# Attention with a gated ReGLU branch on one core: query products of two nested Strassen levels, cut into wider units

## The chip, the core and the metric

The kernel runs on one core of a Trainium2 chip, as one program. Time is the device time of one execution in microseconds (us); a lower one is better. The engines of the core run side by side, each through its own queue in order, and wait for each other by semaphores: TensorE (PE, with its weight loads PEld), VectorE (DVE), ScalarE (ACT), GpSimd (POOL), and SyncE (SP), which only issues transfers.

## What is computed

```python
x = A_x                                        # 1 x 2048 x 512, bfloat16
xn = layernorm(x)
q = (xn @ wq).reshape(1, 2048, 32, 128)        # 32 heads of 128
p = softmax(q k_cache^T * 128 ** -0.5)         # per head, 2048 cached keys
s = concat_heads(p v_cache) @ wo               # 2048 x 512
gate = xn @ W_gate; up = xn @ W_up             # 512 x 1792
g = silu((gate * (gate > 0) * up) @ W_down)    # 2048 x 512
out = x + s * g
```

## The kernel before

**Attention loop.** Work is ordered by pairs. A *pair* is two tiles of 128 keys against 512 queries of one head: two score matmuls (L1455, 512 columns each) into a two-bank PSUM slot, one exponential on ScalarE over both (L1467), and eight value matmuls (L1564, 129 columns) that accumulate into `ps_acc`. Eight pairs make a *block* (one head, one quarter Q of the queries), four blocks a head, and four heads a *group*: 16 blocks, 8 groups, 128 blocks in all. In the text r is a block's place in its group of 16, 0 to 15, and p0 to p7 are the pairs of a block. TensorE issues the scores of a pair three pairs ahead of its value matmuls (`LAG`). Value matmuls wait for the exponential of their pair. At the end of a block VectorE normalises (L1484, L1487), and SP issues the transpose of the result into `OT_store` (L1492); the first value matmul of the next block waits for the normalisation.

**Ring.** PSUM has three slots of two banks (`ps_r`, `NSLOT`). `ring_acquire` takes them in turn for score pairs and for all other products, and TensorE waits until the last reader of a slot is done: the exponential, or VectorE. A slot can be held (`hold=True`): it then leaves the turn until `ring_release` puts it back as second next, with the tokens that its next user waits for.

**Side work.** What else has to be done is hung on pairs by tables at the end of the program: `plan` (TensorE work of a pair, put between its score matmuls and its value matmuls) and `side` (work of other engines, emitted after it). In a pair without `plan` work the order is one score matmul, four value matmuls, the other score matmul, four value matmuls. The side work of the steady groups is:
- Output projection of the group before (`emit_os`, products on L1336, additions into `s_acc` on L1354): one step in p0 of each block; steps of two products in three blocks of four, and in r = 3, 7, 11, 15 a step of one product, where the scores of the next pair are pulled ahead of it (`early`). Before it, VectorE forms four sums of `OT_store` into `OX` twice a group: in r=0, p2 to p5, and in r=7, p1 to p4 (`emit_ox`, L1305 to L1313). GpSimd prepares `Wo` (`emit_wx`, L1278 and L1289 to L1294) in r=6, p0.
- Query projection of the next group. Heads are projected four at a time by Strassen's scheme applied twice: seven outer products (j = 1 to 7), each again by seven inner ones. The outer order is 1, 2, 6, 5, 3, 7, 4. A *unit* is one outer product for half of the columns (c = 0 or 1): seven matmuls of 256 columns (L1030). There are 14 units a group, for groups 2 to 7; groups 0 and 1 are projected by the one-level scheme (`emit_st`).

**A unit.** GpSimd forms the inner sums ahead (`prep_unit`, L1005): four tiles T of the activations, of the tile set TI, and four tiles X of the weights, of SI; it waits until the unit two before is done, whose tiles these are. Then five steps in consecutive pairs p3 to p7 of one block, on one held slot with banks A and B (`emit_unit`): TensorE writes a product into A or B, mostly accumulating onto what stands there, and VectorE reads the bank in between and adds it to the running sums UU, VV, RR (L1035, or a copy on L1034) or writes finished query tiles to `QT_sb`. The next product into a bank waits for that reading. At step 1 one read of A goes into two quarters at once (`to_broadcast`), except in units 1 and 5, which start new sums. The units j=5 and j=7 are followed by sums on GpSimd (`add_unit`, L1098 and L1104), which the next unit's first addition waits for.

**Weights.** `load_unit_w`, `scale_unit_w` and `sum_unit_w` bring and prepare the weights of a group in r = 2 and 4 (L979 to L991).

**Gate.** The gated branch is computed at the start, beside the first 16 blocks; its result g stands in `g_sb` (16 KB a partition) until the last group, where `emit_base` (from block 117 on, L1432 and L1437) multiplies and adds the input tiles that `issue_xr` has loaded from block 116 on.

**Start.** The first products of the one-level scheme (`emit_st`, pr=0, c=1, step 0) are read out by a copy on ScalarE (L908), since ScalarE is used there and VectorE elsewhere (L911); the result goes on to L898.

Of the kernel before, what the change touches and what calls it, by code (L numbers as in the profile page):

```python
# [52 lines left out]
def bass_recurrent_scan__mha_block_cached__glu_gated_reglu__prompt_kernel(  # L53
# [63 lines left out]
    with ExitStack() as es:  # L117
# [18 lines left out]
        xnT = S_([128, DC, S], BF16, "xnT")  # L136
        g_sb = S_([128, NT, D], BF16, "g_sb")
# [112 lines left out]
        sem_ui = newsem()  # L250
        sem_up = newsem()
# [15 lines left out]
        sem_qpa = newsem()  # L267
# [605 lines left out]
        def emit_st(pr, c, step, *banks):  # L873
# [26 lines left out]
            if step == 0:  # L900
                _wait(pe, sw_tok[(pr, 0)])
                if pr == 0 and c == 0:
                    _wait_all(pe, xt_ready[0])
                p1 = prod(1, banks[0])
                p2 = prod(2, banks[1])
                if pr == 0 and c == 1:
                    _wait_all(act, [p1, st_tok["r"]])
                    st_tok["u"] = sem_qpa.sig(act.copy(cu[:], ps_r[:, banks[0], :]))  # L908
# [29 lines left out]
        unit_order = (1, 2, 6, 5, 3, 7, 4)  # L938
        unit_at = []
# [17 lines left out]
        def outer_x(j, i, c, r):  # L957
            a = c * NQ + r * HQ
            if j == 1:
                return xnT[:, i, a:a + HQ]  # L960
            if j == 2:
                return xnT[:, HC + i, a:a + HQ]
            if j == 3:
                return xnT[:, HC + i, HS + a:HS + a + HQ]
            return TX[:, {5: 0, 6: 1, 7: 2, 4: 3}[j], i, a:a + HQ]

        def load_unit_w(g, i):
# [3 lines left out]
            else:  # L971
                _wait(sp, u_done[(g - 1, 1, 4 if i else 2)])
# [8 lines left out]
        def sum_unit_w(g):  # L981
            _wait(pool, wu_tok[(g, 1)])
            _wait(pool, u_done[(g - 1, 1, 7)] if g > 2 else qp_done_tok[3])
# [9 lines left out]
        def prep_unit(n):  # L993
            g, c, j, _ = unit_at[n]
            T, X = TI[n % 2], SI[n % 2]
            if n >= 2:
                _wait(pool, u_done[unit_at[n - 2][:3]])
# [3 lines left out]
            b11, b12 = outer_x(j, 0, c, 0), outer_x(j, 0, c, 1)  # L1001
            b21, b22 = outer_x(j, 1, c, 0), outer_x(j, 1, c, 1)
# [4 lines left out]
            k1 = op(T[:, 0], b12, b11)  # L1007
            k2 = op(X[:, 0], a21, a22, ALU.add)
            op(T[:, 2], b22, b12)
            op(X[:, 2], a11, a21)  # L1010
            _wait(pool, k1)
            k3 = op(T[:, 1], b22, T[:, 0])
# [3 lines left out]
            op(T[:, 3], b21, T[:, 1])  # L1016
# [3 lines left out]
        def emit_unit(n, step):  # L1020
            g, c, j, _ = unit_at[n]
# [18 lines left out]
            outs = {2: (0, c), 3: (0, c + QB // 2), 4: (2, c)}.get(j)  # L1040
            k = u_tok

            def out(i):
# [3 lines left out]
                hq = (G * g + outs[0] + e, outs[1])  # L1047
                if hq not in qt_slot:
                    qt_take(*hq)
                return QT_sb[qt_slot[hq]][:, r * HQ:(r + 1) * HQ]  # L1050

            def outdone(tok):
                if outs is not None:
                    for e in range(2):
                        qt_ready[(G * g + outs[0] + e, outs[1])] = tok

            if step == 0:
                p1 = mm(A, outer_w(j, 0, 0), outer_x(j, 0, c, 0), True, False)
                p6 = mm(B, X[:, 1, :], T[:, 1, :], True, False)
# [6 lines left out]
            elif step == 1:  # L1066
                _wait(pe, k["b"])
                p5 = mm(B, X[:, 0, :], T[:, 0, :], False, False)
# [3 lines left out]
                else:  # L1072
                    k["b"] = dv(D[3], base[:, 3, :], B, p5)
                    k["a"] = dv(dest[:, 2:4, :], dest[:, 2:4, :],
                                ps_r[:, 2 * s:2 * s + 1, 0:HQ].to_broadcast([128, 2, HQ]), k["b"])
            elif step == 2:
                _wait(pe, k["b"])
                p3 = mm(B, X[:, 3, :], outer_x(j, 1, c, 1), False, True)
                k["b"] = dv(out(1), D[1], B, p3, k["a"])
            elif step == 3:  # L1080
                _wait(pe, k["a"])
                p2 = mm(A, outer_w(j, 1, 0), outer_x(j, 1, c, 0), False, True)
                _wait(pe, k["b"])
                p7 = mm(B, X[:, 2, :], T[:, 2, :], True, False)
                k["b"] = dv(out(3), D[3], B, p7, k["a"])
                k["a"] = dv(out(0), None if base is None else base[:, 0, :], A, p2)
            else:
                _wait(pe, k["b"])
                p4 = mm(B, outer_w(j, 1, 1), T[:, 3, :], False, True)
                u_done[(g, c, j)] = p4  # L1090
                k["last"] = dv(out(2), D[2], B, p4, k["a"])
# [3 lines left out]
        def add_unit(g, c, j):  # L1095
            _wait(pool, u_tok["last"])
            if j == 5:
                u_tok["add"] = sem_uv.sig(pool.tensor_tensor(VV[:], UU[:], RR[:], ALU.add))  # L1098
                return
            for e in range(2):  # L1100
# [738 lines left out]
```

## Time and profile before

| | us |
|---|---|
| median of three runs | 1244.05 |
| their range | 1243.62 to 1244.43 |
| the profiled execution, its time | 1243.37 |
| the profiled execution, its span | 1242.0 |
| TensorE busy | 1224.3 |
| ScalarE busy | 1032.0 |
| VectorE busy | 858.9 |
| GpSimd busy | 694.4 |
| granted TensorE clock, mean | 1.0 |

The span is the time from the first to the last instruction. In the views below a row is a group of like instructions or, in the timeline, a run of them on one engine: start, time from its first start to its last end, engine, line, operation, tiles written and read, shapes and count; brackets give the idle time of the engine before it and what ended that. Matmuls are pipelined: the time from one start to the next is what one costs, and their own durations overlap. A busy time of TensorE therefore doesn't say how much it could still take.

### The profile page before, as it was taken

What the parts mean: (1) busy time and instruction counts of PE and PEld (TensorE: products, weight loads), DVE (VectorE), ACT (ScalarE), POOL (GpSimd) and SP (SyncE); (2) the same over time, 40 slices, a digit from 0 to 9 for tenths busy, and PEclk for the clock granted to TensorE, in tenths of its full rate; (3) what the DMA queues carried; (4) which work ended last, traced back from release to release, by engine and by line L of the source; (5) the groups of instructions that cost most, each with busy time, mean ns of one, the idle gap of its engine ahead of it and who ended that gap; (6) DMA issues with size and microseconds to landing.
All of it is one profiled execution on the core that took longest, in us unless ns stands there. A gap on an engine that the chain in (4) does not pass through costs nothing.

```text
span 1242.0 us, 30671 instructions
## 1 busy us (share of the span) xinstructions
PE 1224.3 (99%) x12413; PEld 890.9 (72%) x12647; DVE 858.9 (69%) x1664; ACT 1032.0 (83%) x1109; POOL 694.4 (56%) x930
## 2 busy tenths in 40 slices
PE   9999999999999999999999999999999999999998
PEld 5466666777777777777777777777777777777775
DVE  7677778666666766776766667667666676666667
ACT  4457877667898898988988988998989989889994
POOL 3383876414645578547864687457863796550002
PEclk9999999999999999999999999999999999999999
DMA  9712331221222232233122332242222223434312
GB/s 275 157 31 36 77 81 23 52 48 35 49 48 52 65 70 53 48 69 61 43 37 48 73 61 53 48 69 66 51 52 52 53 48 48 53 69 74 77 36 77
DMA packets 250699, 78.14 MB, mean 63 GB/s; under 512 B 226240, under 2 KB 250560, under 8 KB 250560
## 3 DMA queue, kind: packets, MB, share of 16 engines
q1 hardware_dynamic: 249888, 75.79, 31.2%
q8 instruction: 100, 1.64, 0.6%
q10 hardware_dynamic: 672, 0.39, 0.1%
q14 instruction: 39, 0.32, 0.1%
HBM read 38.54 MB, written 2.10 MB: 33 GB/s over the span
## 4 chain that ended last, share of the span: by engine, by line
PE 87%; issue 8%; ACT 3%; DVE 1%; POOL 1%; POOLq 0%; DVEq 0%
PE ps_acc L1564 33%; PE ps_r L1455 29%; PE ps_r L1336 6%; PE ps_r L1030 6%; PE ps_r L1133 3%; ACT PT L1467 3%; PE ps_r L1194 3%; PE ps_r L708 2%; PE ps_r L712 2%; PE ps_r L893 2%; PE ps_acc L811 1%; DVE UVR L1035 1%; POOL g_sb L1619 1%; PE ps_r L459 0%; PE ps_r L525 0%
## 5 line engine op out<-in xcount | busy, mean ns | idle before, releaser
L1467 ACT ACTIVATE PT<-ps_r 128x1024 bf16<-128x1024 f32 x1024 | 980.6, 1030 | 141.2 <-PE ps_r L1455 129.8
L1564 PE MATMUL ps_acc<-V_sb,PT 128*128 128x129 bf16 x8192 | 688.3, 220 | 5.4
L1564 PEld LDWEIGHTS ps_acc<-V_sb,PT 128*128 128x128 bf16 x8192 | 574.9, 98 | 145.2 <-ACT PT L1467 2.9
L1455 PE MATMUL ps_r<-QT_sb,KT_sb 128*128 128x512 bf16 x1823 | 600.8, 379 | 5.3 <-DVE QT_sb L898 0.3
L1035 DVE TENSOR_TENSOR UVR<-UVR,ps_r 128x256 f32<-128x256 f32 (+1 forms) x456 | 198.3, 455 | 160.8 <-PE ps_r L1030 156.1
L1354 DVE TENSOR_TENSOR s_acc<-s_acc,ps_r 128x512 f32<-128x512 f32 x264 | 167.8, 683 | 15.2 <-PE ps_r L1336 15.2
L1455 PEld LDWEIGHTS ps_r<-QT_sb,KT_sb 128*128 128x128 bf16 x2048 | 171.7, 98 | 7.6 <-ACT PT L1467 0.5
L1005 POOL TENSOR_TENSOR TI<-xn_sb 128x256 f16<-128x256 f16 x96 | 66.2, 689 | 89.0 <-PE ps_r L1030 88.1
L1487 DVE TENSOR_TENSOR Onorm<-ps_acc,rz_sb 128x512 bf16<-128x512 f32 x127 | 87.8, 692 | 4.4
L1098 POOL TENSOR_TENSOR UVR<-UVR,UVR 128x1024 f32<-128x1024 f32 x12 | 28.3, 2361 | 99.2 <-DVE UVR L1035 99.2
L1035 DVE TENSOR_TENSOR QT_sb<-UVR,ps_r 128x256 bf16<-128x256 f32 x144 | 57.4, 419 | 28.2 <-PE ps_r L1030 23.4
L1030 PE MATMUL ps_r<-TI,SI 128*128 128x256 f16 x252 | 68.7, 273 | 0.0
L1005 POOL TENSOR_TENSOR TI<-xn_sb,TI 128x256 f16<-128x256 f16 x96 | 67.6, 704 | 0.0
L1619 POOL TENSOR_TENSOR g_sb<-s_acc,WX 128x512 bf16<-128x512 f32 x6 | 6.8, 1155 | 108.0 <-DVE WX L1612 108.0
L1005 POOL TENSOR_TENSOR TI<-xnT 128x256 f16<-128x256 bf16 x72 | 50.7, 704 | 28.0 <-PE ps_r L1030 28.0
L1484 DVE RECIPROCAL rz_sb<-ps_acc 128x4 f32<-128x4 f32 x127 | 23.2, 183 | 61.7 <-PE ps_acc L1564 59.0
L979 POOL TENSOR_SCALAR Wq_sb<-Wq_sb 128x1024 bf16<-128x1024 bf16 x12 | 33.2, 2770 | 48.2 <-DMA Wq_sb<-in_A_wq_dram 46.9
L1104 POOL TENSOR_TENSOR QT_sb<-UVR,UVR 128x512 bf16<-128x512 f32 x24 | 30.1, 1276 | 38.7 <-DVE UVR L1035 38.7
L1034 DVE COPY UVR<-ps_r 128x256 f32<-128x256 f32 x72 | 28.2, 419 | 33.6 <-PE ps_r L1030 33.6
L1005 POOL TENSOR_TENSOR TI<-xnT,TI 128x256 f16<-128x256 bf16 x72 | 50.7, 704 | 0.0
L1030 PEld LDWEIGHTS ps_r<-TI,SI 128*128 128x128 f16 x252 | 24.3, 97 | 34.1 <-DVE QT_sb L1035 6.8
L1005 POOL TENSOR_TENSOR SI<-SO 128x128 f16<-128x128 f16 x96 | 48.6, 506 | 0.0
(186 smaller groups left out, 1342.7 us busy)
## 6 DMA issues: line engine op xcount, KB each, us to landing
V_sb<-in_A_v_cache_dram SPq DMA_DIRECT2D x32, 512.0 KB, 4.5
Wq_sb<-in_A_wq_dram SPq DMA_DIRECT2D x16, 256.0 KB, 3.2
Wo_sb<-in_A_wo_dram SPq DMA_DIRECT2D x8, 512.0 KB, 4.8
xr_sb<-in_A_x_dram SPq DMA_DIRECT2D x16, 128.0 KB, 2.0
OT_store<-Onorm SPq DMA_TRANSPOSE x127, 2.5
Wd_sb<-in_B_W_down_dram SPq DMA_DIRECT2D x1, 1792.0 KB, 14.1
W<-in_B_W_gate_dram SPq DMA_DIRECT2D x14, 128.0 KB, 2.4
W<-in_B_W_up_dram SPq DMA_DIRECT2D x14, 128.0 KB, 2.8
```

Of the source, the lines that this page charges most:

```text
L979: wu_tok[(g, i)] = sem_uo.sig(pool.tensor_scalar(w, w, WSC, None, op0=ALU.mult))
L1005: return sem_ui.sig(pool.tensor_tensor(dst, x, y, o))
L1030: return sem_up.sig(pe.matmul(dst, lhs, rhs, start=start, stop=stop, skip_group_check=True))
L1035: dve.tensor_tensor(dst, x, ps, ALU.add))
L1133: ins = pe.matmul(ps_r[:, bank, :], L(i), R(i), start=(i == 0), stop=(i == HC - 1))
L1194: ins = pe.matmul(ps_r[:, bank, j * DH:(j + 1) * DH], L(i), R(i), start=(i == 0 and j == 0), stop=(i == HF - 1 and j == 1))
L1336: ins = pe.matmul(ps_r[:, bank, j * DH:(j + 1) * DH], L(i), R(i), start=(i == 0 and j == 0), stop=(i == GH - 1 and j == 1))
L1354: t = dve.tensor_tensor(names[k], names[k], view(bank), op)
L1455: ins = pe.matmul(ps_r[:, 2 * s + tt, :], KT_sb[h % 2][:, t * 128:(t + 1) * 128], QT_sb[qt_slot[(h, Q)]][:], start=True, stop=True)
L1467: act.activation(PT[pb][:], ps_r[:, 2 * s:2 * s + 2, :], ACTF.Exp, scale=scale / WSC)
L1487: dve.tensor_tensor(Onorm[ob][:], o_ap, rz_sb[:].to_broadcast([128, 4, Dh]), ALU.mult))
L1564: ins = pe.matmul(o_ap, PT[pb][:, tt, j * 128:(j + 1) * 128], V_sb[vb][:, t, 0:VW], start=(t == 0 and j % 2 == 0), stop=(t == KT - 1 and j ...
```

## The change

A unit now covers both halves of the columns: 7 units a group instead of 14, with seven matmuls of 512 columns. It is spread over two blocks: steps 0 to 3 in p2, p4, p5 and p6 of r = 6, 8, ..., 18, with five matmuls, and steps 4 and 5 in p2 and p4 of the next block, with one each; each part has a held slot of its own. (r = 16, 17, 18, 19 are r = 0 to 3 of the next group.) UU, VV and RR are twice as large. UU and VV take the place of `g_sb`; so the gate values are written out to the output's memory in block 17 and read back from block 115 on, after the last unit. The four inner tiles T are separate tiles; GpSimd's sums after j=5 and j=7 are four of 512 columns, and their place is p5 of the second block. Preparation stands two blocks ahead of its unit instead of one, `emit_wx` in r=8, p6, and the weight sums in r=4, p3 instead of p6. The copy at the start is on VectorE.

```diff
+        g_at = (nc.sbuf_base + 31) // 32 * 32
         g_sb = S_([128, NT, D], BF16, "g_sb")
...
-        HQ = NQ // 2
-        UU, VV, RR = (at_(o, [128, 4, HQ], F32, "UVR") for o in (104448, 96256, 92160))
-        TI = [at_(o, [128, 4, HQ], F16, "TI") for o in (65536, 100352)]
+        UU, VV, RR = (at_(o, [128, 4, NQ], F32, "UVR") for o in (g_at - base[0], g_at - base[0] + 8192, 92160))
+        TI = [[at_(o, [128, NQ], F16, "TI") for o in os_] for os_ in (
+            (104448, 105472, 106496, 107520), (65536, 66560, 100352, 101376))]
...
-                if pr == 0 and c == 1:
-                    _wait_all(act, [p1, st_tok["r"]])
-                    st_tok["u"] = sem_qpa.sig(act.copy(cu[:], ps_r[:, banks[0], :]))
-                else:
-                    _wait(dve, p1)
-                    st_tok["u"] = sem_qpe.sig(dve.tensor_copy(cu[:], ps_r[:, banks[0], :]))
+                _wait(dve, p1)
+                st_tok["u"] = sem_qpe.sig(dve.tensor_copy(cu[:], ps_r[:, banks[0], :]))
...
-        for g in range(2, NG):
-            bs = ([21, 22, 24, 25, 26, 27, 28, 29, 30, 31, 32, 33, 34, 35] if g == 2 else
-                  [GBK * (g - 1) + r for r in (4, 5, 6, 8, 9, 10, 11, 12, 13, 14, 15, 17, 18, 19)])
-            unit_at += [(g, k // 7, unit_order[k % 7], b) for k, b in enumerate(bs)]
+        unit_at = [(g, j, GBK * (g - 1) + 6 + 2 * k) for g in range(2, NG)
+                   for k, j in enumerate((1, 2, 6, 5, 3, 7, 4))]
...
+            if step in (0, 4):
+                u_held[n] = ring_acquire(hold=True)
             if step == 0:
-                u_held[n] = ring_acquire(hold=True)
                 _wait(pe, u_prep[n])
+                if n == 0:
+                    _wait(dve, sem_gs.cur())
             s = u_held[n]
-            A, B = ps_r[:, 2 * s, 0:HQ], ps_r[:, 2 * s + 1, 0:HQ]
+            A, B = ps_r[:, 2 * s, :], ps_r[:, 2 * s + 1, :]
...
                 else:
                     k["b"] = dv(D[3], base[:, 3, :], B, p5)
                     k["a"] = dv(dest[:, 2:4, :], dest[:, 2:4, :],
-                                ps_r[:, 2 * s:2 * s + 1, 0:HQ].to_broadcast([128, 2, HQ]), k["b"])
+                                ps_r[:, 2 * s:2 * s + 1, :].to_broadcast([128, 2, NQ]), k["b"])
...
             elif step == 3:
                 _wait(pe, k["a"])
-                p2 = mm(A, outer_w(j, 1, 0), outer_x(j, 1, c, 0), False, True)
-                _wait(pe, k["b"])
-                p7 = mm(B, X[:, 2, :], T[:, 2, :], True, False)
-                k["b"] = dv(out(3), D[3], B, p7, k["a"])
+                p2 = mm(A, outer_w(j, 1, 0), outer_x(j, 1, 0), False, True)
                 k["a"] = dv(out(0), None if base is None else base[:, 0, :], A, p2)
+                ring_release(u_held.pop(n), [k["b"], k["a"]])
+            elif step == 4:
+                p7 = mm(B, X[:, 2, :], T[2][:], True, False)
+                k["b"] = dv(out(3), D[3], B, p7)
             else:
                 _wait(pe, k["b"])
-                p4 = mm(B, outer_w(j, 1, 1), T[:, 3, :], False, True)
-                u_done[(g, c, j)] = p4
-                k["last"] = dv(out(2), D[2], B, p4, k["a"])
+                p4 = mm(B, outer_w(j, 1, 1), T[3][:], False, True)
+                u_done[(g, j)] = p4
+                k["last"] = dv(out(2), D[2], B, p4)
                 outdone(k["last"])
                 ring_release(u_held.pop(n), [k["last"]])
...
+        def spill_g():
+            _wait_all(sp, [sem_dg.cur(), sem_g.cur()])
+            for Q in range(QB):
+                sem_gs.sig(sp.dma_start(out_t[:, 4 * Q:4 * Q + 4, :], g_sb[:, 4 * Q:4 * Q + 4, :]))
+
+        def reload_g():
+            _wait_all(sp, [u_tok["last"], sem_gs.cur()])
+            for Q in (0, 2, 1, 3):
+                sem_gr[Q].sig(sp.dma_start(g_sb[:, 4 * Q:4 * Q + 4, :], out_t[:, 4 * Q:4 * Q + 4, :]))
...
-            _wait(dve, sem_dg.cur())
+            _wait(dve, sem_gr[n // 4].cur())
...
-        for n, (g, c, j, b) in enumerate(unit_at):
-            for step, p in enumerate((3, 4, 5, 6, 7)):
-                at(b, p, (emit_unit, 0, n, step))
-            side.setdefault((b - 1, 0), []).append((prep_unit, n))
+        for n, (g, j, b) in enumerate(unit_at):
+            for step, (r, p) in enumerate(((0, 2), (0, 4), (0, 5), (0, 6), (1, 2), (1, 4))):
+                at(b + r, p, (emit_unit, 0, n, step))
+            side.setdefault((b - 2, 0), []).append((prep_unit, n))
             if j in (5, 7):
-                side.setdefault((b, 7), []).append((add_unit, g, c, j))
+                side.setdefault((b + 1, 5), []).append((add_unit, g, j))
+        side.setdefault((GB + 1, 0), []).append((spill_g,))
+        side.setdefault((LB - 9, 5), []).append((reload_g,))
...
-            b, p = (22, 4) if g == 2 else (b, 6)
+            b, p = (22, 4) if g == 2 else (b, 3)
...
-            if pq == 0 and bq % GB == 6 and 1 < bq // GB < NG - 1:
+            if pq == 6 and bq % GB == 8 and 1 < bq // GB < NG - 1:
                 emit_wx(bq // GB)
```

More of the change, by code (lines that the diff above doesn't have):

```diff
@@ L250, in bass_recurrent_scan__mha_block_cached__glu_gated_reglu__prompt_kernel @@
         sem_ui = newsem()
+        sem_gs = newsem(16)
+        sem_gr = [newsem(16) for _ in range(QB)]
         sem_up = newsem()
@@ L1046, in out @@
                 e, r = divmod(i, 2)
[L1047 to L1050, printed above, removed]
+                return qt_take(G * g + outs[0] + e, outs[1] + r)
             def outdone(tok):
                 if outs is not None:
-                    for e in range(2):
-                        qt_ready[(G * g + outs[0] + e, outs[1])] = tok
+                    for i in range(4):
+                        qt_ready[(G * g + outs[0] + i // 2, outs[1] + i % 2)] = tok
             if step == 0:
-                p1 = mm(A, outer_w(j, 0, 0), outer_x(j, 0, c, 0), True, False)
-                p6 = mm(B, X[:, 1, :], T[:, 1, :], True, False)
+                p1 = mm(A, outer_w(j, 0, 0), outer_x(j, 0, 0), True, False)
+                p6 = mm(B, X[:, 1, :], T[1][:], True, False)
                 if base is None:
```

62 lines of the change are left out of this document (30 added, 32 removed).

## The prediction

> **What bounds the kernel now.** I read the page's busy times first, then the chain of waits, then the timeline of TensorE through two blocks.
>
> ```profile
> span 1242.0 us, 30671 instructions
> PE 1224.3 (99%) x12413; PEld 890.9 (72%) x12647; DVE 858.9 (69%) x1664; ACT 1032.0 (83%) x1109; POOL 694.4 (56%) x930
> ...
> PE 87%; issue 8%; ACT 3%; DVE 1%; POOL 1%; POOLq 0%; DVEq 0%
> ```
>
> TensorE is busy 99%. That alone proves little, since the ends of matmuls are modelled; whether it has slack is read from start to start (columns: start us, us from the first start to the last end):
>
> ```profile
> 687.58 0.27 PE L1030 MATMUL ps_r<-TI,SO 128*128 128x256 f16 x1
> 687.69 0.62 PE L1564 MATMUL ps_acc<-V_sb,PT 128*128 128x129 bf16 x8
> 688.15 0.59 PE L1455 MATMUL ps_r<-QT_sb,KT_sb 128*128 128x512 bf16 x2
> 688.58 1.04 PE L1336 MATMUL ps_r<-Wo_sb,OT_store 128*128 128x256 bf16 x8
> ...
> 690.35 0.38 PE L1455 MATMUL ps_r<-QT_sb,KT_sb 128*128 128x512 bf16 x1
> ...
> 696.10 0.59 PE L1455 MATMUL ps_r<-QT_sb,KT_sb 128*128 128x512 bf16 x2
> ...
> 704.82 0.59 PE L1455 MATMUL ps_r<-QT_sb,KT_sb 128*128 128x512 bf16 x2
> ```
>
> Two score matmuls take 688.58-688.15 = 0.43, so 0.216 each; a 256-wide product takes 687.69-687.58 = 0.11 (eight 256-wide output products, 0.27 + 7 x 0.109 = 1.04); eight value matmuls 688.15-687.69 = 0.46, 0.057 each. A plain pair is then 0.88. A block of 16 score and 64 value matmuls with eight output products sums to 7.95. The block r=0, which has no unit, runs from 688.15 to 696.10: 7.95. The next has a unit, seven 256-wide matmuls, +0.76: 8.72, and 696.10 to 704.82 is 8.72. So TensorE streams with no gap at all in these blocks. Whatever it is made to wait is added to the time, and what other engines save is worth nothing.
>
> **The change, part by part.** *Fewer, wider matmuls.* 588 of 256 columns become 294 of 512. Two narrow ones cost 0.218, a wide one 0.216 (by the rows above): about 0.0027 x 294 = 0.8 us gained. That is the whole direct gain on the engine that bounds.
>
> *The answers between a unit's steps.* A unit is a dialogue: TensorE writes bank A or B, VectorE reads it, and the next product waits for that. Durations (busy us, mean ns):
>
> ```profile
> L1467 ACT ACTIVATE PT<-ps_r 128x1024 bf16<-128x1024 f32 x1024 | 980.6, 1030 | 141.2 <-PE ps_r L1455 129.8 <-remote 4.7
> L1035 DVE TENSOR_TENSOR UVR<-UVR,ps_r 128x256 f32<-128x256 f32 x396 | 157.1, 419 | 158.7 <-PE ps_r L1030 156.1
> L1035 DVE TENSOR_TENSOR UVR<-UVR,ps_r 128x512 f32<-128x512 f32 x60 | 41.2, 687 | 2.0
> L1098 POOL TENSOR_TENSOR UVR<-UVR,UVR 128x1024 f32<-128x1024 f32 x12 | 28.3, 2361 | 99.2 <-DVE UVR L1035 99.2
> L1005 POOL TENSOR_TENSOR SI<-Wq_sb 128x128 f16<-128x128 bf16 x72 | 31.0, 431 | 0.0
> L987 POOL TENSOR_TENSOR SO<-Wq_sb 128x512 f16<-128x512 bf16 x6 | 6.9, 1157 | 0.0
> ```
>
> A 512-wide addition takes 0.687 instead of 0.419, and VectorE starts the next independent one 0.60 later (row 689.22 below: (1.88-0.69)/2). The 1024-wide one, one read of A into two quarters, is not in the trace. Bounds: 0.92, the r=0 operation of 1024 fp16 elements at 691.02, and 1.29, two 512-wide ones in a row. I take 1.22 (419 to 687 is 268 ns per 256 columns, twice more). Latencies:
>
> ```profile
> 68.67 0.59 PE L893 MATMUL ps_r<-xn_sb,Wq_sb 128*128 128x512 f16 x2
> 69.30 0.69 DVE L898 TENSOR_TENSOR QT_sb<-cuv,ps_r 128x512 bf16<-128x512 f32 x1 [0.18 <-PE ps_r L893]
> ...
> 420.39 0.75 DVE L1035 TENSOR_TENSOR UVR<-UVR,ps_r 128x256 f32<-128x256 f32 x2
> 420.85 0.10 PEld L1030 LDWEIGHTS ps_r<-xn_sb,SI 128*128 128x128 f16 x1 [0.39 <-DVE UVR L1035]
> 420.86 0.28 PE L1030 MATMUL ps_r<-xn_sb,SI 128*128 128x256 f16 x1
> 421.05 0.68 DVE L1310 TENSOR_TENSOR OX<-OX,OT_store 128x1024 f16<-128x1024 f16 x1
> ...
> 690.76 1.94 ACT L1467 ACTIVATE PT<-ps_r 128x1024 bf16<-128x1024 f32 x2 [0.96 <-PE ps_r L1455]
> ```
>
> The second 512-wide matmul starts at 68.67+0.216 and its reader at 69.30: 0.42. The first addition of 420.39 ends at 420.81, the product that waited starts at 420.86: 0.055. The score matmul of 690.35 is followed by its exponential at 690.76, also 0.41, and the next exponential comes 1.94-1.03 = 0.91 later: ScalarE could do a block in 7.3 us and is not the limit.
>
> Now the first half of a unit, in the time of its block (start 0). Pair 0 has the output products and takes 1.76, pair 1 ends at 2.64, step 0 puts A at 3.07 and B at 3.29 (the previous output additions end at 2.95, just in time for its slot). Step 1 writes B at 5.27; its addition runs 5.69 to 6.38; step 2 could start one pair of 1.10 later, 6.37, but may at 6.43: **0.06 lost**, in each of six units of a group. The 1024-wide addition follows from 6.41 to 7.63; step 3 could start at 7.53, but may at 7.69: **0.16 lost** in the four units with a base (2, 6, 3, 4; units 1 and 5 have a 512-wide one there). The narrow version needed 0.11+0.20+0.42+0.055 = 0.79 for the first of these, under its pair of 0.99. The slot is free at 9.02, the next block asks at 9.24. 6 x 0.06 + 4 x 0.16 = 1.0 us a group.
>
> *The block r=0.* Unit 7 now has its first half where the four OX sums stand on VectorE, and where no unit stood before but once:
>
> ```profile
> 689.22 1.88 DVE L1354 TENSOR_TENSOR s_acc<-s_acc,ps_r 128x512 f32<-128x512 f32 x3
> 691.02 0.92 DVE L1305 TENSOR_TENSOR OX<-OT_store 128x1024 f16<-128x1024 bf16 x1
> 691.86 0.91 DVE L1307 TENSOR_TENSOR OX<-OT_store 128x1024 f16<-128x1024 bf16 x1
> 692.69 1.15 DVE L1310 TENSOR_TENSOR OX<-OX,OT_store 128x1024 f16<-128x1024 f16 x1
> ```
>
> VectorE's queue there: two additions from 3.71, OX 1 and 2 from 4.91, step 1's addition, the 1024-wide one, OX 3, step 2's addition, OX 4, step 3's. An OX sum takes 0.68 alone (421.05), 0.91 to 1.15 beside GpSimd's preparations. The preparation of the last unit starts when unit 3's last product frees its tiles, in the fifth pair of r=15, and takes 4 x 1.16 + 4 x 0.43 = 6.4, so it ends about 3.7, ahead of the first OX sum: I take 0.68. Then step 1's addition ends at 6.80 (step 2 loses 0.48), the 1024-wide one at 8.06 (step 3 loses 0.16), step 3's at 10.46, and the next block's first score matmul, which takes the slot that the half gives back, starts at 10.51 instead of 9.66: 0.85. Sum **1.5 a group**; with the slow OX sums the same count gives 2.6. Block r=7 has OX sums too, beside a second half, with two additions: the last ends 0.3 ahead of the matmul that takes its slot, so nothing is lost; beside a working GpSimd it is 0.8.
>
> *A wait at each fourth block.* In r=3, 7, 11, 15 the second score pair is pulled ahead of the output products, and these take the slot of the preceding pair 7. Formerly that pair had a unit step and issued both score matmuls at its start; now it is plain, the second 0.23 later. Its exponential ends at 0.44+0.42+1.02, +0.055 = 1.94 from that pair's start; the output products could start at 0.88+0.86 = 1.75: **0.19**, and 0.03 at the unit's slot just behind: 0.9 a group.
>
> *GpSimd.* Its additions after units 5 and 7 become four of 512, 2361/2 = 1.18 each or somewhat more: done 5 us after the half ends, 0.9 us ahead of the first addition of the next unit. Nothing, but if it comes late, VectorE waits there with the unit's second addition, the next output additions and the normalisation queued behind it. The output weights' preparation (L1278 and four sums), moved from r=6 to r=8 on GpSimd's queue, is first read at r=0, eight blocks on; it takes some 10 us, ends in r=9, ahead of the preparation for r=12. The other moved weight steps have two blocks to spare. The query slots that a unit takes were given back at least two blocks earlier, so those waits cost nothing.
>
> *The gate values.* 2 MB go out at the start of block 17 and come back from block 115:
>
> ```profile
> 1133.55 2.00 SPq L1425 DMA_DIRECT2D xr_sb<-in_A_x_dram  x4
> ...
> 1141.48 0.69 DVE L1437 TENSOR_TENSOR s_acc<-s_acc,xr_sb 128x512 f32<-128x512 f32 x1
> ```
>
> ```profile
> V_sb<-in_A_v_cache_dram SPq DMA_DIRECT2D x32, 512.0 KB, 4.5
> ```
>
> The way out has five blocks, some 43 us, for four transfers of 4.5 at most each (18 us); on SP the transposes of OT_store and the key loads stand behind them, with four blocks of slack. VectorE's new wait, ahead of the first unit in block 22, is long over. On the way back SP waits for the last unit, one addition, with a V load, a transpose and the xr loads behind it; they now have 7.9 us between issue and use, of which the transfers may take 8 to 18. A late load holds VectorE in block 117 where 5 us remain before TensorE needs it. I take nothing; bound 0 to 8 us.
>
> *The PSUM copy.* It stood on ScalarE, and its reader and then TensorE waited:
>
> ```profile
> 73.23 0.69 DVE L898 TENSOR_TENSOR QT_sb<-cuv,ps_r 128x512 bf16<-128x512 f32 x1 [1.35 <-ACT cuv L908]
> ...
> 74.07 0.59 PE L1455 MATMUL ps_r<-QT_sb,KT_sb 128*128 128x512 bf16 x2 [0.30 <-DVE QT_sb L898]
> ```
>
> VectorE is idle there; 0.3 us gained. The one old unit that met OX sums stalled too (420.85); I count 0.1 for that.
>
> **Sum.** A group loses 1.0 + 1.5 + 0.9 = 3.4; six groups (2 to 7) 20.1; less 0.8, 0.3 and 0.1: +18.9. The profiled execution took 1243.37 (span 1242.0), the median 1244.05: 1262.3 and 1262.9. I say 1262.5.
>
> **Rivals.** *Locked OX sums.* If GpSimd's preparations do run beside them (a late start of 1.2 us suffices), r=0 costs 2.6 and r=7 0.8: 1.9 more a group, 1274. For it: in the trace of before they did overlap. Against: the preparation now starts earlier than the block. SBUF — State Buffer, "Who interferes with whom", of the Trainium skill says that a VectorE operation with two SBUF inputs is blocked for the whole of a GpSimd instruction that reads SBUF. By that rule the wide preparations, 1.16 a piece, would block an OX sum longer than the narrow ones did; the trace agrees, with 0.68 alone and 1.15 beside GpSimd.
>
> *The stalls fall into waits paid anyway.* The chain gives TensorE only 87%; if the other 13% were slack in each block (1.1 us of 8.7), the 3.4 a group would vanish in the 14 blocks of its units, and the time would be 1242.0, within 0.2% of before. It decides once slack a block exceeds 0.25. Against: the sums of start-to-start times equal the blocks' times to 0.01.
>
> *Wide matmuls that stream closer.* At a spacing of 0.13 instead of 0.216 the 294 products gain 25 us more: 1237; from 0.152 the sum is below before. Against: both widths in the rows above. TensorE: Matmul & The Clock Gate, "Back-to-back issue gap", of the Trainium skill gives 131 ns as the sustained spacing at 512 columns. The trace disagrees: 0.216.
>
> *Shorter answers.* If the 1024-wide addition takes 0.92, step 3 loses nothing and r=0 0.9: 3.4 becomes 2.1, and the time 1255.
>
> *Late GpSimd or gate values.* Additions 1 us late in 12 places and 8 us at the reload: 1280.
>
> **Chances.** Forecast 0.58 (its own range 1257 to 1268), shorter answers 0.12, locked OX sums 0.14, late work 0.05, no loss 0.10 (1242.0, give or take 3 for work that merely shifts: half of it faster by over 0.2%, half within), closer streaming 0.01. What this measurement can tell from no change is 0.2%, 2.5 us. Range 1251 to 1276: it holds the three cases in the middle. Faster 0.06, same 0.05, slower 0.89.
>
> **What would show it.** In the profile after: blocks of r=1 starting some 10.5 us after r=0, with the first score matmul released by a VectorE addition to UVR; weight loads of the unit's second and third steps released by VectorE, 0.06 and 0.16 late; output products of r=3, 7, 11, 15 released by the exponential; OX sums at 0.68. Wrong if unit blocks add up to the plain sum of matmuls, or if a wait stands on the reload or on GpSimd's sums.

## The result, and the profile after

| | before | after |
|---|---|---|
| median, us (six runs each, side by side) | 1243.55 | 1265.55 |
| range, us | 1243.33 to 1244.43 | 1265.36 to 1265.57 |
| ratio after/before, 95% interval | | 1.0175 [1.0162, 1.0188] |
| profiled execution, time / span, us | 1243.37 / 1242.0 | 1265.56 / 1264.2 |

The change costs 22.0 us; the prediction was 1262.5, in a range of 1251 to 1276. The page after, busy times and the chain of waits:

```profile
span 1264.2 us, 29137 instructions
PE 1238.9 (98%) x12124; PEld 856.6 (68%) x12353; DVE 804.9 (64%) x1329; ACT 1033.6 (82%) x1108; POOL 588.5 (47%) x606
...
PE 80%; issue 8%; ACT 7%; DVE 3%; POOL 0%; DMA 0%; POOLq 0%; DVEq 0%
```

VectorE and GpSimd have less to do than before, 54 and 106 us; neither was the bound, and the time went up. The chain has moved from TensorE (87 to 80%) to ScalarE and VectorE: TensorE now waits for answers. The busy share (99 to 98%) hardly tells it.

Where the time went is told by the groups, each measured from the first exponential of its first pair to that of the next group (the last one to the end of its last exponential), in the profiled executions:

| group of 16 blocks | 0 | 1 | 2 | 3 | 4 | 5 | 6 | 7 |
|---|---|---|---|---|---|---|---|---|
| before | 202.22 | 141.19 | 137.21 | 136.20 | 136.30 | 136.21 | 136.20 | 134.27 |
| after | 202.20 | 143.54 | 139.89 | 139.89 | 139.89 | 139.90 | 139.89 | 136.55 |
| difference | -0.02 | 2.35 | 2.69 | 3.69 | 3.59 | 3.69 | 3.69 | 2.28 |

The loss is the same, 3.6 to 3.7, in groups 3 to 6; groups 1 and 7, which hold only some of a group's units, lose less, and group 0, which has no unit, loses nothing. (Group 2 had one narrow unit more before, and group 7 has it now: 0.76 belongs to the one instead of the other.) The differences, and 0.2 by which the first exponential came later in this execution, give the 22.2 between the spans. Lengths of blocks below are counted in the same way, from first exponential to first exponential.

The timeline after around a block r=0, in which unit 7 has its first half:

```profile
699.09 0.42 POOL L999 TENSOR_TENSOR SI<-Wq_sb,SI 128x128 f16<-128x128 bf16 x1
701.29 0.68 DVE L1311 TENSOR_TENSOR OX<-OT_store 128x1024 f16<-128x1024 bf16 x1
701.66 0.38 PE L1027 MATMUL ps_r<-TI,SI 128*128 128x512 f16 x1
702.37 0.59 PE L1461 MATMUL ps_r<-QT_sb,KT_sb 128*128 128x512 bf16 x2
702.50 1.93 DVE L1032 TENSOR_TENSOR UVR<-UVR,ps_r 128x512 f32<-128x512 f32 x2
703.24 0.39 PE L1027 MATMUL ps_r<-xn_sb,SI 128*128 128x512 f16 x1 [0.27 <-DVE UVR L1032]
704.49 0.39 PE L1027 MATMUL ps_r<-xn_sb,SO 128*128 128x512 f16 x1
...
706.15 0.68 DVE L1032 TENSOR_TENSOR UVR<-UVR,ps_r 128x512 f32<-128x512 f32 x1
706.88 0.11 PEld L1461 LDWEIGHTS ps_r<-QT_sb,KT_sb 128*128 128x128 bf16 x2 [0.85 <-DVE UVR L1032]
707.12 0.38 PE L1461 MATMUL ps_r<-QT_sb,KT_sb 128*128 128x512 bf16 x1 [0.90 <-DVE UVR L1032]
```

Step 1 asks at 701.66. VectorE starts the answer at 702.50, after two OX sums, so step 2 starts at 703.24, 0.44 after the two score matmuls ahead of it have passed (702.37 + 2 x 0.216). Step 3 at 704.49 is 0.14 late, and the next block's first score matmul can start only when VectorE's last addition has given the slot back: 706.15 + 0.68 = 706.83, and its weights load at 706.88. The row of TensorE names 707.12 with one matmul, but two loads stand at 706.88: the record of the first of the pair is missing, and the wait is 0.85, by the row of the loads.

The same view after, from unit 4's first half in r=2 to the output products of r=3:

```profile
720.14 3.95 ACT L1473 ACTIVATE PT<-ps_r 128x1024 bf16<-128x1024 f32 x4 [0.26 <-PE ps_r L1461]
720.82 0.62 PE L1570 MATMUL ps_acc<-V_sb,PT 128*128 128x129 bf16 x8
721.31 0.59 PE L1461 MATMUL ps_r<-QT_sb,KT_sb 128*128 128x512 bf16 x2
721.76 0.39 PE L1027 MATMUL ps_r<-xn_sb,SI 128*128 128x512 f16 x1
...
724.55 1.94 ACT L1473 ACTIVATE PT<-ps_r 128x1024 bf16<-128x1024 f32 x2 [0.46 <-PE ps_r L1461]
724.58 1.03 PE L1461 MATMUL ps_r<-QT_sb,KT_sb 128*128 128x512 bf16 x4
725.63 0.61 PE L1342 MATMUL ps_r<-WX,OT_store 128*128 128x256 f16 x4
```

The score matmuls at 721.31 are 0.04 late: the eight value matmuls ahead of them start at 720.82 and take 0.45, to 721.27. Their slot is free when the first exponential of the row at 720.14 is done, at 721.16. Step 2 (721.76) is 0.02 behind its score matmuls. Four score matmuls from 724.58 take 0.86, to 725.44; the output products wait until 725.63, which is the end of the first of the two exponentials, 724.55 + 1.02, and 0.06: 0.19 lost, as worked out.

Three groups of the view by lines, shapes kept apart (busy us, mean ns):

```profile
L1032 DVE TENSOR_TENSOR UVR<-UVR,ps_r 128x512 f32<-128x512 f32 x198 | 131.6, 685 | 88.6 <-PE ps_r L1027 86.8
L1032 DVE TENSOR_TENSOR UVR<-UVR,ps_r 128x1024 f32<-128x1024 f32 x30 | 36.6, 1220 | 1.0
L1098 POOL TENSOR_TENSOR UVR<-UVR,UVR 128x512 f32<-128x512 f32 x24 | 29.8, 1272 | 73.3 <-DVE UVR L1032 73.3
```

The 1024-wide addition takes the 1.22 that the prediction took between 0.92 and 1.29. GpSimd's sums take 1.27 instead of 1.18, and no wait on them shows on VectorE.

### The profile page after: what moved, and what is told of

It is laid out like the page before. It is cut to its first block, busy times and chain, and to the rows that moved or that the text cites. A ratio compares the mean times of both kernels' runs of the same rounds, so it can differ in the third digit from the quotient of the medians.

```text
span 1264.2 us, 29137 instructions
## 1 busy us (share of the span) xinstructions
PE 1238.9 (98%) x12124; PEld 856.6 (68%) x12353; DVE 804.9 (64%) x1329; ACT 1033.6 (82%) x1108; POOL 588.5 (47%) x606
## 4 chain that ended last, share of the span: by engine, by line
PE 80%; issue 8%; ACT 7%; DVE 3%; POOL 0%; DMA 0%; POOLq 0%; DVEq 0%
PE ps_acc L1570 31%; PE ps_r L1461 26%; ACT PT L1473 7%; PE ps_r L1027 6%; PE ps_r L1342 6%; PE ps_r L1139 3%; PE ps_r L1200 2%; PE ps_r L710 2%; PE ps_r L714 2%; PE ps_r L895 2%; DVE UVR L1032 1%; PE ps_acc L813 1%; POOL g_sb L1625 0%; DVE OX L1319 0%; DVE OX L1313 0%
## 5 line engine op out<-in xcount | busy, mean ns | idle before, releaser
L1032 DVE TENSOR_TENSOR UVR<-UVR,ps_r 128x512 f32<-128x512 f32 (+1 forms) x228 | 168.2, 755 | 89.7 <-PE ps_r L1027 86.8
L999 POOL TENSOR_TENSOR TI<-xn_sb 128x512 f16<-128x512 f16 x48 | 55.3, 1153 | 113.3 <-PE ps_r L1027 113.3
L999 POOL TENSOR_TENSOR TI<-xnT 128x512 f16<-128x512 bf16 x36 | 41.5, 1154 | 69.6 <-PE ps_r L1027 68.8
L1032 DVE TENSOR_TENSOR QT_sb<-UVR,ps_r 128x512 bf16<-128x512 f32 x72 | 47.9, 686 | 36.6 <-PE ps_r L1027 34.2
L1098 POOL TENSOR_TENSOR UVR<-UVR,UVR 128x512 f32<-128x512 f32 x24 | 29.8, 1272 | 73.3 <-DVE UVR L1032 73.3
L999 POOL TENSOR_TENSOR TI<-xn_sb,TI 128x512 f16<-128x512 f16 x48 | 55.4, 1154 | 0.0
L1027 PE MATMUL ps_r<-TI,SI 128*128 128x512 f16 x126 | 48.0, 381 | 0.6
L1342 PE MATMUL ps_r<-WX,OX 128*128 128x256 f16 x336 | 45.8, 273 | 0.0
L999 POOL TENSOR_TENSOR TI<-xnT,TI 128x512 f16<-128x512 bf16 x36 | 41.6, 1157 | 0.0
L1115 POOL TENSOR_SCALAR gB<-gB 128x512 bf16<-128x512 bf16 x14 | 20.8, 1487 | 42.4 <-DVE gB L1145 42.4
L1342 PEld LDWEIGHTS ps_r<-WX,OX 128*128 128x128 f16 x336 | 32.9, 98 | 9.8 <-ACT PT L1473 1.8
```

The costliest lines, as they stand in the source:

```text
L999: return sem_ui.sig(pool.tensor_tensor(dst, x, y, o))
L1027: return sem_up.sig(pe.matmul(dst, lhs, rhs, start=start, stop=stop, skip_group_check=True))
L1032: dve.tensor_tensor(dst, x, ps, ALU.add))
L1098: u_tok["add"] = sem_uv.sig(pool.tensor_tensor(dst, UU[:, i, :], RR[:, i, :], ALU.add))
L1342: ins = pe.matmul(ps_r[:, bank, j * DH:(j + 1) * DH], L(i), R(i), start=(i == 0 and j == 0), stop=(i == GH - 1 and j == 1))
```

## The experiments

All are edits of the changed kernel except two, of the kernel before. Ratios are to runs of the kernel before on the same chip.

**ox_away: the OX sums off the block r=0.**

```diff
-                    side.setdefault((b0 + 7 * c, (2, 1)[c] + i), []).append((emit_ox, g, c, i))
+                    b, p = (b0 + 7 * c, (2, 1)[c] + i) if c or g == 0 else (b0 - 1, (3, 5, 6, 7)[i])
+                    side.setdefault((b, p), []).append((emit_ox, g, c, i))
```

> The changed kernel, with the first four OX sums of a group taken off the block r=0 and put into the block before it (r=15, pairs p3, p5, p6, p7), for groups 2 to 7. My theory: VectorE's queue in r=0 is what delays unit 7's first half there, so the 1.64 us lost around r=0 (0.44 at step 2, 0.14 at step 3, 1.06 at the next block's first score matmul) falls to the 0.2 of the other units: 1.45 x 6 = 8.7 us less, 1256.9. Rival 1: it is the 1024-wide addition and the slot order that hold the next block's score matmul, and the sums only stand there: only step 2's 0.42 goes, 1263. Rival 2: beside GpSimd's preparations the sums are slowed to 0.9 to 1.15 each and hold unit 3's second half in r=15: half the gain, 1261.

Measured: 1265.0, ratio 1.017 [1.0153, 1.0187]: almost nothing gained. Its timeline in r=15 and the start of r=0:

```profile
692.77 1.15 POOL L999 TENSOR_TENSOR TI<-xn_sb 128x512 f16<-128x512 f16 x1 [5.82 <-PE ps_r L1027]
692.81 1.66 DVE L1311 TENSOR_TENSOR OX<-OT_store 128x1024 f16<-128x1024 bf16 x1 [1.32 <-DMA OT_store<-Onorm]
693.88 0.87 POOL L999 TENSOR_TENSOR SI<-Wq_sb 128x128 f16<-128x128 bf16 x1
694.39 0.67 DVE L1032 TENSOR_TENSOR QT_sb<-UVR,ps_r 128x512 bf16<-128x512 f32 x1
...
694.99 1.42 DVE L1313 TENSOR_TENSOR OX<-OT_store 128x1024 f16<-128x1024 bf16 x1
695.12 0.39 PE L1461 MATMUL ps_r<-QT_sb,KT_sb 128*128 128x512 bf16 x1 [1.06 <-DVE QT_sb L1032]
...
699.77 0.61 PE L1570 MATMUL ps_acc<-V_sb,PT 128*128 128x129 bf16 x8 [1.40 <-DVE Onorm L1493]
```

Two things are to be seen. The waits around r=0 did go, but for the small ones that every unit has: from the first exponential of r=1 to that of r=2 it is 9.24 us, not 10.50. But the sums, 0.68 each in r=0 of the changed kernel, take 1.66 and 1.42 beside GpSimd's preparation, and TensorE waits behind them at two new places, for a slot that VectorE holds (695.12) and for the normalisation (699.77). This place is the worst of six: its first sum waits 1.32 for a transpose, and so meets the preparation too. At four of the others the first sum waits for nothing and takes 0.68, the other three take 1.07, 0.91 and 1.53, and TensorE waits only for the normalisation, 0.85 late:

```profile
836.76 1.53 DVE L1319 TENSOR_TENSOR OX<-OT_store,OX 128x1024 f16<-128x1024 bf16 x1
839.25 0.61 PE L1570 MATMUL ps_acc<-V_sb,PT 128*128 128x129 bf16 x8 [0.69 <-DVE Onorm L1493]
```

There 1.26 is gained and 0.85 lost; at the place shown first the loss is 2.79. The addition at 694.39, which has one input in PSUM and one in SBUF, keeps its 0.67, though GpSimd works. SBUF — State Buffer, "Who interferes with whom", of the Trainium skill has this as a lock: VectorE with two SBUF inputs, and GpSimd reading SBUF, block each other for a whole instruction, and one SBUF input alone is free of it. These rows agree, in both halves.

**ox_clear: the same, with GpSimd held back.** The sums stand in r=15, p5 to p7, and in p1 of r=0, and the preparation that ran beside them waits for the last one.

```diff
+                    b, p = (b0 + 7 * c, (2, 1)[c] + i) if c or g == 0 else ((b0 - 1, 5), (b0 - 1, 6), (b0 - 1, 7), (b0, 1))[i]
...
+            if j == 4:
+                _wait(pool, ox_tok[(g - 1, 0)])
...
-            side.setdefault((b - 2, 0), []).append((prep_unit, n))
+            side.setdefault((b - 2, int(j == 4)), []).append((prep_unit, n))
```

> The changed kernel, with the four OX sums in r=15, pairs p5, p6, p7, and in p1 of r=0, and with GpSimd's preparation of unit 4 (the one for r=2) waiting until the last of them is done. My theory: moved to r=15 beside that preparation, the sums took 0.91 to 1.66 and gave the 1.64 a group back at other places; kept apart from it they take 0.68 and the gain stays: 1.45 x 6 = 8.7 less than the changed kernel, 1256.9, with r=1's block at 9.24 and r=0's at 8.44. Rival 1: the sums are slow in r=15 because of what VectorE and the transfers do there, not because of GpSimd: 1263 to 1265. Rival 2: the preparation, 6.4 long and now starting some 7 later, comes late for r=2: 1258 to 1262, with TensorE waiting on GpSimd there.

Measured: 1257.92, ratio 1.0117 [1.0102, 1.0132], 7.6 less than the changed kernel. Its timeline (two lines of code more than above, so L1029 there is L1027 of the changed kernel):

```profile
691.44 0.68 DVE L1313 TENSOR_TENSOR OX<-OT_store 128x1024 f16<-128x1024 bf16 x1
692.04 0.68 DVE L1315 TENSOR_TENSOR OX<-OT_store 128x1024 f16<-128x1024 bf16 x1
...
696.58 0.68 DVE L1321 TENSOR_TENSOR OX<-OT_store,OX 128x1024 f16<-128x1024 bf16 x1
697.43 1.16 POOL L1001 TENSOR_TENSOR TI<-xn_sb 128x512 f16<-128x512 f16 x1 [12.46 <-PE ps_r L1029]
```

The sums are back at 0.68, and the blocks are 8.44 and 9.24, as expected. The gain is 1.26 a group, not the 1.45 expected: that had taken the 1.06 of the missing record for the wait. So the stall of r=0 is VectorE's queue. This edit changed the places of the sums and GpSimd's work at once; that the earlier failure was GpSimd's neighbourhood is read from the two traces: each moved sum over 0.69 has GpSimd at work beside it for its whole length, and all those of ox_clear, with nothing beside them, take 0.68.

**os_scores: both score matmuls first in the plain pair ahead of r = 3, 7, 11, 15.**

```diff
+            soon = not items and not ahead and pq == 7 and bq + 1 in early
+            if soon:
+                emit_S_tile(gp, 1)
...
-            if not items and not ahead:
+            if not items and not ahead and not soon:
                 emit_S_tile(gp, 1)
```

> The changed kernel, with both score matmuls of the plain pair p7 ahead of its value matmuls where the next block is r = 3, 7, 11 or 15. My theory: the output products there wait for the exponential of that pair, 0.19 late, and the unit's slot behind it 0.046: (0.19 + 0.046) x 4 x 6 = 5.6 us less, 1259.9. Rival 1: the wait passes to the next exponential or to VectorE's release of the same ring slots, and nothing is gained: 1265.5. Rival 2: the row names the exponential, but it was VectorE that was late: no change in the wait either.

Measured: 1259.96, ratio 1.0133 [1.0118, 1.0148], 5.6 less. The timeline of the kernel, where the output products of r=3 stood 0.19 late:

```profile
721.96 1.03 PE L1461 MATMUL ps_r<-QT_sb,KT_sb 128*128 128x512 bf16 x4
722.82 0.60 PE L1342 MATMUL ps_r<-WX,OT_store 128*128 128x256 f16 x4
```

They follow the four score matmuls with no gap (4 x 0.216 = 0.86), and each such block is 0.23 shorter. The exponential was the cause.

**step1_p3: a pair more between a unit's steps 1 and 2.**

```diff
-                p1 = mm(A, outer_w(j, 0, 0), outer_x(j, 0, 0), True, False)
                 p6 = mm(B, X[:, 1, :], T[1][:], True, False)
+                p1 = mm(A, outer_w(j, 0, 0), outer_x(j, 0, 0), True, False)
...
-            for step, (r, p) in enumerate(((0, 2), (0, 4), (0, 5), (0, 6), (1, 2), (1, 4))):
+            for step, (r, p) in enumerate(((0, 2), (0, 3), (0, 5), (0, 6), (1, 2), (1, 4))):
```

> The changed kernel, with a unit's step 1 in p3 instead of p4, and bank B written ahead of A in step 0 so that its answer comes first. My theory: step 3 waits for the 1024-wide addition, 0.142 late, in four units of a group; with one pair more between them that wait goes: 0.57 x 6 = 3.4 us less. In r=0 VectorE is busy without a break and hands the slot back at about the same time, so of 1.64 only some 0.2 goes: 1.2 more. Together 1261. Rival 1: answers are limited by VectorE's rate and not by the one pair of room, so an earlier question gets no earlier answer: 1265.5. Rival 2: step 1 itself now waits for step 0's answer, 0.06 to 0.14 in each of seven units: 1264 to 1267.

Measured: 1257.98, ratio 1.0117 [1.0102, 1.0132], 7.6 less where 4.6 were expected. In the trace no step of a unit waits any more. The rest, as far as it was found, is small change elsewhere: eight of fourteen waits of 0.04 (see plain_scores) and the 0.02 at step 2 are gone too, together 0.4 a group. In r=0 the slot still comes late. The end of that block in its timeline:

```profile
701.68 0.39 PE L1570 MATMUL ps_acc<-V_sb,PT 128*128 128x129 bf16 x4
702.43 0.68 DVE L1032 TENSOR_TENSOR UVR<-UVR,ps_r 128x512 f32<-128x512 f32 x1
703.39 0.38 PE L1461 MATMUL ps_r<-QT_sb,KT_sb 128*128 128x512 bf16 x1 [1.32 <-DVE UVR L1032]
```

The score matmuls are due at 701.91 (701.68 and four value matmuls of 0.057). VectorE's last addition ends at 703.11, and the first of the pair, whose record is missing again, must have started 0.216 ahead of 703.39, at 703.17: 1.26 late, where the three waits of r=0 came to 1.42. VectorE's rows, from the unit's first answer at 696.37 to 703.11, follow each other without a break. Asking earlier helps where the answer's latency is the limit, not where the engine that answers is full.

**two_adds: the 1024-wide addition as two of 512.**

```diff
-                    k["a"] = dv(dest[:, 2:4, :], dest[:, 2:4, :],
-                                ps_r[:, 2 * s:2 * s + 1, :].to_broadcast([128, 2, NQ]), k["b"])
+                    dv(D[2], D[2], A, k["b"])
+                    k["a"] = dv(D[3], D[3], A)
```

> The changed kernel, with the 1024-wide addition of step 1 as two additions of 512 columns. My theory: VectorE needs 0.60 + 0.69 = 1.29 for the two instead of 1.22, and TensorE's step 3 waits for that answer in five units of a group (j = 2, 6, 7, 3, 4), so its stall there goes from 0.142 to 0.21: 0.07 x 5 x 6 = 2.1 more, 1267.7. Rival: the wait is not for the duration of this addition but for something else that ends then: 1265.5. Rival 2: two separate additions cost more between them than two of a row: 1269 or more.

Measured: 1267.45, ratio 1.0193 [1.0175, 1.0211], 1.9 more than the changed kernel. Its timeline:

```profile
721.95 2.01 DVE L1032 TENSOR_TENSOR UVR<-UVR,ps_r 128x512 f32<-128x512 f32 x3 [0.70 <-PE ps_r L1027]
723.37 0.59 PE L1461 MATMUL ps_r<-QT_sb,KT_sb 128*128 128x512 bf16 x2
724.01 0.39 PE L1027 MATMUL ps_r<-xn_sb,Wq_sb 128*128 128x512 f16 x1
```

Three additions end at 723.96, step 3 starts at 724.01, 0.21 late instead of 0.14: the stall follows the duration of the answer.

**plain_scores: both score matmuls first in the plain pair p3.** The edit is that of os_scores, with the condition `pq == 3 and bq > GB + 5` in place of the one on p7.

> The changed kernel, with both score matmuls of each plain pair p3 ahead of its value matmuls (after block 22). My theory: the score matmul of p5 waits 0.040 at 14 places a group for the exponential of that plain pair, whose second score matmul comes 0.23 late; without that 0.56 a group goes, and step 2, which profits from the wait ahead of it (0.02 instead of the 0.06 worked out), loses 0.04 more in seven units: 0.56 - 0.28 = 0.28 a group, 1.7 in all, 1263.9. Rival 1: the 0.040 belongs to something else (the slot's order, a matmul that is longer here): 1265.5, and the gaps stay. Rival 2: step 2 does not lose it back: 1262.2.

Measured: 1263.97, ratio 1.0167 [1.0149, 1.0185], 1.6 less. Its timeline:

```profile
720.35 0.59 PE L1461 MATMUL ps_r<-QT_sb,KT_sb 128*128 128x512 bf16 x2
720.84 0.39 PE L1027 MATMUL ps_r<-xn_sb,SI 128*128 128x512 f16 x1
```

The waits of 0.04 are gone, and step 2 is now 0.06 late (720.84 - 720.35 - 0.43), the figure of the prediction. In the changed kernel the one wait hid most of the other.

**all3 and all_clear: the edits together.** The first has ox_away, step1_p3, and both score matmuls first in every plain pair after block 22; the second has ox_clear in place of ox_away.

> The changed kernel with the three edits together (OX sums in r=15, step 1 in p3 with B first, both score matmuls first), the last of them in every plain pair after block 22. My theory: the losses are separate terms and add up: 8.7 + 5.6 + 3.4, and 0.04 x 13 x 6 = 3.1 for the score matmuls that wait behind a plain pair, 20.8 less: 1244.7, with no wait of TensorE on UVR left in the profile. Rival 1: behind each wait stands another nearly as late, and the gains overlap: 1250 to 1255. Rival 2: the change's cost lies elsewhere (wider matmuls, gate values): 1260 or more.

> The kernel of the three edits together, with the OX sums placed and GpSimd held as in the kernel before it. My theory: all that was left of the change's losses is about 1.0 a group at r=15 and r=0, so 1250.8 - 6 = 1244.8, 0.1% above the kernel before: then TensorE streams without a wait in all steady blocks, and the change itself is worth nothing either way. Rival 1: the two kinds of edit collide (step 1's early answers queue behind OX sum 4 in p1), 1247 to 1250. Rival 2: it falls below the kernel before by the 0.8 that the wide matmuls save: 1242.6.

Measured: 1250.79, ratio 1.0058 [1.0043, 1.0073], and 1243.26, ratio 0.9998 [0.9989, 1.0007]. The first falls short by the sums that GpSimd slows: around its block r=0 TensorE still waits 0.89 for the normalisation, and in two of the six groups the first sum waits for a transpose besides (1.77 and 1.16). The second has all 22.3 back, against the single gains 7.6 + 5.6 + 7.6 = 20.8 and some of the waits of 0.04. Its page, and the timeline of a block r=0:

```profile
PE 90%; issue 7%; DVE 1%; POOL 1%; DMA 0%; ACT 0%; SPq 0%; POOLq 0%; DVEq 0%
```

```profile
690.28 0.38 PE L1029 MATMUL ps_r<-TI,SI 128*128 128x512 f16 x1
690.50 0.38 PE L1029 MATMUL ps_r<-xn_sb,SO 128*128 128x512 f16 x1
...
693.15 0.59 PE L1463 MATMUL ps_r<-QT_sb,KT_sb 128*128 128x512 bf16 x2
693.58 0.38 PE L1029 MATMUL ps_r<-xn_sb,SI 128*128 128x512 f16 x1
...
696.24 0.59 PE L1463 MATMUL ps_r<-QT_sb,KT_sb 128*128 128x512 bf16 x2
696.67 1.04 PE L1344 MATMUL ps_r<-WX,OX 128*128 128x256 f16 x8
```

Step 2 (693.58) stands 0.43 behind its score matmuls, and the next block's output products (696.67) 0.43 behind theirs: no gap. A steady group takes 136.20, as before the change. It can't be told from the kernel before: without its waits the change is worth about nothing, as the stream of TensorE is as long with either.

**gate_before and copy_before: two parts alone, put into the kernel before.** The first adds `spill_g` and `reload_g` (in block 115, p7) and the wait of `emit_base` on them; the second has only the copy on VectorE.

> The kernel before, with the gate values written out in block 17 and read back in block 115 as in the change, though nothing else uses their place. My theory: nobody on the path waits for these transfers: 1243.4, within 0.3. Rival: the xr loads and the transposes behind them on SP come late and hold VectorE in block 117: up to 8 more, 1251.

> The kernel before, with the one PSUM copy on VectorE. The prediction: 0.3 less, 1243.1. My theory now: TensorE comes 0.3 earlier to the next score matmul and loses it again some 8 us later, where it waits for VectorE's projection sums, since VectorE's own chain ends no earlier: 1243.4, with less than 0.15 to be seen. Rival: VectorE, with 0.69 more to do, comes later: 1243.8.

Measured: 1243.56, ratio 1.0001 [0.9992, 1.001], and 1243.36, ratio 0.9999 [0.9989, 1.0009]: neither can be told from nothing.

## Why the prediction was right

**The bound.** TensorE streams without slack, so that each wait adds to the time: confirmed by two_adds, where 0.07 at five places of six groups cost 1.9 (2.1 by the count), and by os_scores, where 0.23 at four places gave 5.6 back. The rival that the stalls fall into waits paid anyway is out.

**The terms.** For a steady group, in us. The measured column is the gap beyond the matmuls' own time in the trace after; the stream without waits is all_clear's group, 136.20, less four waits of 0.02 left in it.

| term | forecast | after | shown by |
|---|---|---|---|
| step 2, six units | 0.36 | 0.12 | plain_scores: 0.06 each once the wait ahead is gone |
| step 3, four units | 0.64 | 0.57 | two_adds, step1_p3 |
| r=0: step 2, step 3, next score matmul | 0.48, 0.16, 0.85 | 0.44, 0.14, 0.85 | ox_clear |
| output products in r = 3, 7, 11, 15 | 0.76 | 0.76 | os_scores |
| the unit's slot behind them | 0.12 | 0.18 | os_scores |
| score matmul behind a plain pair, 14 places | none | 0.56 | plain_scores |
| sum | 3.4 | 3.6 of 3.77 | |

Most of the 0.15 that the table lacks stands behind the waits: the value matmul behind a product that waited starts 0.227 after it instead of 0.216, at 16 places a group (4 of them in all_clear too).

**What was missed.** The prediction followed the unit's answers and the four blocks with an early pair, but not the ordinary score matmul two pairs behind each plain pair while a slot is held. By the same latencies the plain pair's exponential is answered 1.94 after the pair's start, and the score matmul asks at 1.98 (0.88 + 1.10): safe by 0.04. It is late by 0.04. The exponential itself is on time: in r=2 above it ends at 721.16, 1.88 after the pair's first score matmul (719.28). The matmul that takes its slot starts 0.145 later, and not 0.055 as the output products do. It is the first score matmul of a block, for which the program waits for two tokens, the slot's and the query tile's; the trace has a semaphore instruction of TensorE in between, from 721.20 to 721.25, which waits for the exponential, and the weight load behind it, at 721.28, waits for the other token. The 0.145 is the same at all 14 places of a group; that the second token is its cause was not tested. The 14 waits cost 0.56 a group and take 0.24 off step 2 in return: 0.32, or 1.9 in six groups, of the 3.1 between +18.9 and +22.0 (plain_scores gave 1.6 back). The rest is what the table lacks, 0.9, and gains that were forecast and not seen, 0.6, less 0.4 of stalls that came out shorter. That a missed term is partly paid for at step 2 is luck. The step that fell short is "A group loses 1.0 + 1.5 + 0.9 = 3.4": the kind was right, and one term was left out. Two sums of the prediction are a little off, without weight for the forecast: six groups of 3.37 are 20.2, not 20.1, and late work, 12 places of 1 us and 8, gives 1282.5, not 1280.

**The 1.1 to be gained.** Of the 0.8 for wide matmuls some 0.5 can be worked out: a steady group without waits would be 0.08 shorter than before (136.12 against 136.20). No run shows it, since all_clear has four waits of 0.02 left in a group. The 0.3 of the copy was seen and lost. The start, after, first VectorE, then TensorE:

```profile
72.26 0.69 DVE L909 COPY cuv<-ps_r 128x512 f32<-128x512 f32 x1 [0.17 <-PE ps_r L895]
73.06 0.69 DVE L900 TENSOR_TENSOR QT_sb<-cuv,ps_r 128x512 bf16<-128x512 f32 x1
73.81 0.60 PE L1461 MATMUL ps_r<-QT_sb,KT_sb 128*128 128x512 bf16 x2
...
82.04 0.60 PE L895 MATMUL ps_r<-xnT,SW 128*128 128x512 bf16 x2 [0.17 <-DVE cuv L900]
```

The wait of 0.30 ahead of 73.81 is gone, and 8 us on TensorE waits for VectorE, where it did not before: 82.04 is 0.34 behind the score matmuls ahead of it (81.27 + 2 x 0.216), of which the row counts 0.17. In copy_before's trace that second wait is absent, its block 0 is 0.4 shorter, and its first exponential 0.4 later than in the kernel before; so the second wait, the reason that its expectation gives, is not there, and what becomes of the 0.3 stays open at this size.

**OX sums not locked.** The prediction put the end of GpSimd's preparation ahead of the first OX sum, and so it is: the last of it ends at 699.51, the sum starts at 701.29 and takes 0.68. In r=7 it was not so: there the fourth sum takes 1.15 beside GpSimd (763.73 in the trace after), as it does in groups 1 to 6, but no wait of TensorE comes of it. The rival was not idle fancy: in ox_away, 8.5 us earlier, the sums of r=0 met that preparation, and at more than the 1.15 of its price.

**Gate values at nothing.** Right, by gate_before. In the changed kernel the `xr` loads stand behind the transfers back on SP and come late; VectorE waits 0.68 for one, and TensorE does not wait for VectorE there:

```profile
1151.17 2.18 SPq L1110 DMA_DIRECT2D g_sb<-out_dram  x4
...
1161.42 2.01 SPq L1431 DMA_DIRECT2D xr_sb<-in_A_x_dram  x4
...
1164.27 0.69 DVE L1443 TENSOR_TENSOR s_acc<-s_acc,xr_sb 128x512 f32<-128x512 f32 x1 [0.68 <-DMA xr_sb<-in_A_x_dram]
```

**Closer streaming** is out: two wide matmuls of a step start 0.22 apart (690.28 and 690.50 above). The 131 ns that TensorE: Matmul & The Clock Gate, "Back-to-back issue gap", of the Trainium skill gives as sustained at 512 columns are seen in no run here.

## What to carry to other kernels

When the bounding engine streams without a gap, a wider tile on a helper saves the helper's time and lengthens each answer; count for every question and answer the room in the stream against latency plus duration, and for every slot who releases it last, for the plain pairs too. A margin of a few hundredths, worked out from several durations, is no margin when the place repeats 84 times: price it both ways. A matmul that waits for two tokens can start later behind the last of them than one that waits for one. And look at what the neighbouring engine runs before moving work into a gap: the gap at r=15 was free on VectorE and not beside GpSimd.

## What the hardware showed that was not expected

- Beside GpSimd's preparation a VectorE sum of 1024 fp16 elements with both inputs in SBUF took up to 1.66 us instead of 0.68, and GpSimd's own short sums took 0.87 instead of 0.43: both sides pay.
- From the end of an exponential to the output product that waited for it alone it was 0.06 us; to the first score matmul of a block, which waits for a second token as well, 0.145.
- One VectorE addition of 1024 columns, with one bank of PSUM read twice, takes 1.22 us, 1.8 times the 0.685 of one of 512.
